# An attention and expert-layer kernel on one core: products of a cleared tile and a new order of all steps

## The chip, the cores and the metric

The kernel runs on one core of one Trainium2 chip. Five engines with queues of their own take part: TensorE (PE) multiplies matrices, VectorE (DVE), ScalarE (ACT) and GpSimd (POOL) work on tiles, and SyncE (SP) issues all loads and stores. The metric is the device time of one execution in microseconds; lower is better.

## The reference

For 4 batches of 8 heads, 768 tokens and 64 channels per head, each token attends to the keys less than 16 positions away and to 24 summaries of the whole sequence, one per block of 32 tokens (the largest key per channel, the mean of the values). The heads together are the 512 channels of a token mixer of rank 32 and a layer with 2048 hidden units.

```python
k_sum = k.reshape(B, H, nb, block, D).max(axis=3)
v_sum = v.reshape(B, H, nb, block, D).mean(axis=3)
mask_l = np.abs(pos[:, None] - pos[None, :]) < window
scores_s = scale * np.einsum('bhsd,bhnd->bhsn', q, k_sum) + np.log(block)
a = softmax([where(mask_l, scale * q @ k.T, -1e9), scores_s])
x = a @ [v, v_sum]              # (4, 768, 512) over all heads
u = x + ((x.T @ U) @ V).T       # U, V mix the tokens
out = u + np.maximum(u @ w_ch1, 0.0) @ w_ch2
```

U, V and both weight matrices arrive as 64-bit numbers, and the kernel itself turns them into 32-bit ones.

## The kernel before

The four batches follow one another. Each has an attention part and an expert layer, and the attention of batch b+1 is spread over the expert layer of batch b, so that only batch 0's attention stands alone; it is called the opening here.

**Opening.** For each of the 8 heads: load K (`.lk`) and Q (`.lq`, two transfers), take block maxima of K on VectorE (`.K`) and spread them beside the keys (`.Kd` on VectorE, `.Kp` on GpSimd), multiply Q and K by 24 small products on TensorE (`.S`, line 475), take the masked maximum on VectorE (line 500) and the exponential on ScalarE (line 510), six tiles a head (`.E`), transpose on TensorE (`.T`, line 584), copy on ScalarE (`.C`, line 590), multiply by V (`.V`, line 600) and normalise on VectorE (`.N`, lines 628 to 630). Values come in pairs of heads (`.lv`). Block means of V are products (`.M`, line 398), are taken out by ScalarE (`.Mo`) and are spread by copies on GpSimd or VectorE (`.B`, `.D` with p or d; line 438). The queries of heads 4 to 7 are loaded into the places of heads 0 to 3, so their load waits until the scores of that earlier head are done.

**Weights.** A word of 64 bits is scaled on ScalarE (`.X` for U and V, `.Z` and `c` for weights; line 243), turned in three integer steps on GpSimd or VectorE (`.Xt`, `.Y`, `t`; lines 263 to 272), and split into a high and a low part (`.Xs`, `.Xl`, `.W`, `x`; lines 287, 288). `W`, `.la`, `.lb` load a tile of weights.

**Mixer and expert layer.** U and V act through `.I`, `.J`, `.Q`; `.G` forms u for a half of the tokens and a quarter of the channels, and `.Go` takes it out, the high half on ScalarE (line 715), the low half on VectorE (line 716). The first up product (`.U0.0`, line 1018) reads all four of the first half. In batch 0, 16 weight tiles go by two halves of tokens: 12 up products (line 1018), a gate (lines 1030, 1031), and 9 down products (line 1040). The sums of weights that later batches use are formed in this time too (`w`, `d`; lines 872 to 1001) and stored. Batches 1 to 3 use fewer products by a recombination of halves (line 1290), batches 1 and 2 have plain down products (line 1386) and batch 3 a recombined second half (line 1488).

**What sets the order.** It is written out by hand in the text `PLAN`. Its words are steps; each engine's queue takes its instructions in the order of the words and waits only for the data and places that an instruction needs. A `/` ends the list of steps that stands between two groups of products of the expert layer: `body` reads one list after each group. The first list is the whole opening. TensorE's results lie in one of eight banks (`bank`).

```python
    def go():
        for word in next(plan).split():
            name = word.rstrip("0123456789.")
            words_of[name](*map(int, filter(None, word[len(name) :].split("."))))
```

Of the kernel before, what the change touches and what calls it, by code (L numbers as in the profile page):

```python
# [18 lines left out]
P = 128  # L19
# [65 lines left out]
    E1.1.0.1 a1.0.1 S1.1.1 U3 a1.0.1 c1.5 s1.0 E1.1.0.2 E1.1.1.2 t4 E1.1.1.0 t4 W1.6 W0.7
    E1.1.1.1 t4 / f1.0 a1.1.0 x1.3 / k1.3 c1.4 Ka1.2 T1.1 t5 U0 Ba1.0.1 l1.1.1 Ba1.1.1 x0.4 K1.3
    d1.0 / Ba1.0.0 S1.2.0 q1.3 / Ba1.1.0 s1.1 E1.2.0.2 D2 W0.8 W1.7 c0.7 t6 D1 E1.2.0.0 t5 U4
    S1.2.1 E1.2.0.1 q1.4 E1.2.1.1 t7 d1.1 t6 E1.2.1.2 t6 t5 E1.2.1.0 t5 Us1 f1.1 k1.4 t5 / x0.5
    w2.0 / x1.4 P1.0 N1.0 Ka1.3 / S1.3.0 / t6 t6 t6 x1.5 W0.9 a1.1.0 c1.6 c0.8 a1.1.0 t7 t7 T1.2
    Ds1 t8 E1.3.0.1 W1.8 a1.1.0 w2.1 s1.2 / E1.3.0.2 D5 c1.8 v1.3 E1.3.0.0 W1.9 / S1.3.1 q1.5  # L90
    E1.3.1.0 x0.6 k1.5 v1.2 E1.3.1.1 E1.3.1.2 U5 a1.1.0 d2.0 W0.10 t7 c1.7 c0.9 t7 P1.1 N1.1
    K1.4 / T1.3 f1.2 d2.1 a1.1.1 a1.1.0 D3 Ba1.2.1 R1.0 Ka1.4 t7 x0.7 t8 / / / Ba1.2.0 x1.6
    c0.10 c1.9 D6 S1.4.0 E1.4.0.1 U7 w3.0 E1.4.0.0 a1.1.0 t8 K1.5 / / t9 a1.1.1 E1.4.0.2 a1.1.1
    Ka1.5 a1.1.1 t8 r1.0 S1.4.1 E1.4.1.0 E1.4.1.1 P1.2 s1.3 E1.4.1.2 w3.1 Ds2 N1.2 a1.1.1 t8
    W0.11 t8 / / t10 W1.10 t9 t9 a1.1.1 S1.5.0 q1.6 d3.0 g1.0 T1.4 x1.7 x0.8 / E1.5.0.0 E1.5.0.2
    t9 d3.1 E1.5.0.1 / t9 / f1.3 a1.1.1 c0.11 S1.5.1 / Ba1.3.0 t10 Ba1.3.1 Us2 D7 E1.5.1.2
    E1.5.1.0 a1.1.1 s1.4 k1.6 U9 P1.3 E1.5.1.1 W0.12 t10 t9 W1.12 t11 x0.9 N1.3 x1.8 U8 T1.5 t10
    t10 / M1.0 / t10 K1.6 c0.12 R1.1 v1.5 x0.10 D4 w4.0 c1.10 W0.13 Mo1.0 / W1.11 t11 d4.0 J1.0
    x1.9 t12 Jo1.0 t11 c1.12 v1.4 r1.1 D8 t11 w4.1 c1.11 Ka1.6 k1.7 / / S1.6.0 t12 W0.14 t11 t12
    c0.13 E1.6.0.1 E1.6.0.2 a1.1.1 E1.6.0.0 x0.11 Us3 d4.1 t11 / / K1.7 O1.0.0 U10 Ba1.4.1 x1.10  # L100
    / S1.6.1 E1.6.1.2 t12 t13 E1.6.1.1 Ba1.5.1 t13 w5.0 t12 U6 / D10 / E1.6.1.0 t12 g1.1 w5.1
    O1.0.1 f1.4 Ba1.4.0 W1.14 s1.5 t13 O1.0.1 O1.0.1 O1.0.1 x1.11 / c0.14 U11 O1.0.2 d5.0 q1.7
    Ka1.7 t14 d5.1 T1.6 / x0.12 Ba1.5.0 O1.0.1 P1.4 N1.4 / / t13 k2.0 W1.13 c1.13 D11 O1.0.3
    O1.0.3 t13 O1.0.2 O1.0.1 D9 O1.0.2 O1.0.2 Us4 t14 Us5 O1.0.2 O1.0.2 / S1.7.0 c1.14 E1.7.0.0
    E1.7.0.1 W0.15 t13 v1.6 O1.0.2 / Ba1.6.1 s1.6 Ba1.6.0 f1.5 U13 E1.7.0.2 l2.0.0 Ds4 W1.15
    O1.0.3 t14 x1.12 O1.0.3 c0.15 K2.0 / O1.0.2 S1.7.1 O1.0.3 / E1.7.1.1 E1.7.1.0 P1.5 t15 w6.0
    x0.13 t14 E1.7.1.2 O1.0.3 f1.6 t14 T1.7 s1.7 w6.1 / / N1.5 t14 x0.14 c1.15 Kd2.0 x1.13 R1.2
    / Ds3 v1.7 P1.6 t15 k2.1 d6.0 a2.0.0 t15 N1.6 Ba1.7.1 f1.7 / t15 r1.2 t15 t16 Ba1.7.0 t15
    t16 / P1.7 / x1.14 N1.7 M1.2 F F R1.3 g1.2 w7.0 r1.3 t16 Mo1.2 d6.1 Us6 g1.3 p0 / O1.0.2
    J1.2 / p0 a2.0.0 Jo1.2 O1.1.0 p1 p1 x0.15 w7.1 x1.15 D12 p0 / F D15 O1.1.1 O1.1.1 U12 p0  # L110
    O1.1.1 / O1.1.2 p1 O1.1.2 O1.1.1 O1.1.1 l2.0.1 U15 O1.1.2 d7.0 F O1.1.2 / p0 a2.0.0 O1.1.2
    D14 O1.1.1 / O1.1.3 d7.1 O1.1.2 O1.1.3 O1.1.2 O1.1.3 / n0.1 O1.1.2 / O1.1.3 O1.1.3 p1 O1.1.2
    p0 n0.2 q2.0 n0.0 K2.1 a2.0.0 a2.0.0 n1.1 / / n1.2 U14 / a2.0.0 a2.0.1 o0.1 v2.0 D13 q2.1
    a2.0.1 a2.0.0 p1 a2.0.1 Kd2.1 o0.0 o0.2 Us7 O1.1.3 p0 S2.0 Ds5 o0.0 p1 E2.0.0.0 k2.2
# [1540 lines left out]
```

## Time and profile before

| | us |
|---|---|
| median of 3 runs | 630.4 (627.52 to 630.51) |
| the profiled execution | 628.68 |
| its span, from the first to the last instruction | 626.9 |
| busy: TensorE / VectorE / ScalarE / GpSimd | 604.8 / 448.0 / 351.5 / 338.9 |
| first scores begin | 5.62 |
| first up product begins | 50.44 |

The rows of a profile name a line of the kernel, an engine, an operation and what it writes and reads (out<-in) with sizes; `xN` is a count. In a timeline the first number is the start, the second the length of what was merged into the row, and the bracket tells how long the engine was idle before it and what ended that. "PEld" is TensorE's loading of stationary operands, "SPq" the queue of transfers. In the windows each engine has its busy time in a stretch.

### The profile page before, as it was taken

Reading aid. Unit: us, or ns where it says so; the run is one execution under the profiler, and the core shown is the slowest. Engines: PE = TensorE matmul, PEld = TensorE weight load, DVE = VectorE, ACT = ScalarE, POOL = GpSimd, SP = SyncE. Lnnn points to the kernel's source line nnn. Section 1 sums busy time; section 2 is a strip of 40 time slices with the busy share of each in tenths; the row PEclk is TensorE's granted clock in tenths of the full one; section 3 lists DMA queues with packets and bytes.
Section 4 is the critical chain, followed back from the end, with each engine's and each line's share of the span. In section 5 each row is a group of like instructions: output and inputs, shape, how many; then the busy total and the mean of one; then the engine's idle time right before and its main releaser. Section 6 shows DMA issues by size and latency. Waiting matters only on the chain.

```text
span 626.9 us, 14659 instructions
## 1 busy us (share of the span) xinstructions
PE 604.8 (96%) x5360; PEld 551.7 (88%) x5360; DVE 448.0 (71%) x1174; ACT 351.5 (56%) x796; POOL 338.9 (54%) x383
## 2 busy tenths in 40 slices
...
GB/s 231 219 348 248 319 295 290 295 251 282 309 287 242 302 260 284 252 291 250 202 278 174 163 192 235 194 270 211 306 220 263 249 188 123 136 155 264 118 179 64
DMA packets 96838, 147.89 MB, mean 236 GB/s; under 512 B 9472, under 2 KB 67200, under 8 KB 96768
## 3 DMA queue, kind: packets, MB, share of 16 engines
...
HBM read 104.46 MB, written 42.47 MB: 234 GB/s over the span
## 4 chain that ended last, share of the span: by engine, by line
PE 85%; DMA 4%; SPq 3%; DVE 3%; issue 2%; POOL 1%; ACT 1%; DVEq 0%; ACTq 0%; POOLq 0%
PE ps_h L1290 27%; PE acc L1386 19%; PE ps_h L1018 10%; PE acc L1040 9%; PE accx L1488 4%; PE accy L1488 3%; PE accz L1488 3%; PE ps_x L614 2%; PE ps_s L475 2%; DMA place<-in_q 2%; PE ps_s L452 2%; DMA there<-squares 1%; SPq L323 1%; SPq L978 1%; DMA place<-in_w 1%
## 5 line engine op out<-in xcount | busy, mean ns | idle before, releaser
L968 POOL TENSOR_TENSOR parts<-whole,parts 128x512 fp32r<-128x512 f32 (+1 forms) x128 | 158.8, 1253 | 114.4 <-ACT parts L964 98.0
L1290 PE MATMUL ps_h<-place,parts 128*128 128x384 f32 x1008 | 179.9, 336 | 1.0 <-DVE o L1063 0.8
L1290 PEld LDWEIGHTS ps_h<-place,parts 128*128 128x128 f32 x1008 | 174.4, 188 | 3.5 <-DVE o L1063 1.1
L1386 PE MATMUL acc<-gh,parts 128*128 128x256 f32 (+1 forms) x512 | 134.0, 341 | 0.0
L1386 PEld LDWEIGHTS acc<-gh,parts 128*128 128x128 f32 x512 | 88.7, 189 | 12.3 <-issue 1.2
L964 ACT CAST parts<-whole 128x512 fp32r<-128x512 f32 (+1 forms) x144 | 80.4, 581 | 18.3 <-DMA whole<-dsum 5.8
L1386 PE MATMUL acc<-gl,parts 128*128 128x512 f32 (+1 forms) x256 | 86.5, 338 | 0.0
L510 ACT ACTIVATE e<-e,neg 128x120 f32<-128x120 f32 x144 | 51.2, 389 | 42.5 <-DVE neg L500 39.3
L1018 PE MATMUL ps_h<-place 128*128 128x384 f32 x384 | 74.0, 341 | 1.1 <-DVE x L630 0.7
L1018 PEld LDWEIGHTS ps_h<-place 128*128 128x128 f32 x384 | 66.9, 188 | 3.8 <-issue 1.3
L1040 PE MATMUL acc<-place,gh 128*128 128x512 f32 x192 | 66.4, 400 | 0.0
L1359 ACT ACTIVATE gh<-place 128x768 fp32r<-128x768 f32 x32 | 27.1, 846 | 60.6 <-PE acc L1386 60.5
L263 POOL TENSOR_SCALAR val<-place 128x512 f32<-128x512 f32 (+1 forms) x30 | 47.8, 1602 | 21.9 <-ACT place L243 14.7
L288 POOL TENSOR_TENSOR place<-val,place 128x512 fp32r<-128x512 f32 x29 | 39.4, 1366 | 31.0 <-ACT place L287 28.0
L1386 PEld LDWEIGHTS acc<-gl,parts 128*128 128x128 f32 x256 | 48.5, 189 | 4.6 <-DVE gl L1364 0.4
L1364 DVE SCALAR_TENSOR_TENSOR gl<-place,gh 128x768 fp32r<-128x768 f32 x32 | 32.3, 1009 | 27.0 <-ACT gh L1359 27.0
L1040 PEld LDWEIGHTS acc<-place,gh 128*128 128x128 f32 x192 | 36.1, 188 | 7.2 <-ACT gh L1030 0.2
L500 DVE CUSTOM_DVE_ANT_0 e<-ps_s,mask_sb 128x120 f32<-128x120 f32 x144 | 35.1, 275 | 7.8 <-PE ps_s L452 4.4
L1040 PE MATMUL acc<-place,gl 128*128 128x512 f32 x96 | 37.9, 395 | 0.0
L1319 DVE TENSOR_TENSOR place<-place,ps_h 128x384 f32<-128x384 f32 x24 | 13.2, 551 | 28.2 <-PE ps_h L1290 28.1
L744 POOL TENSOR_TENSOR place<-tmp,place 128x384 fp32r<-128x384 f32 x24 | 26.8, 1126 | 11.0 <-ACT place L740 10.8
L530 DVE STREAM_TRANSPOSE squares<-e 128x768 f32<-128x768 f32 x24 | 23.3, 972 | 12.9 <-ACT e L510 8.4
...
## 6 DMA issues: line engine op xcount, KB each, us to landing
...
there<-squares SPq DMA_DIRECT2D x24, 384.0 KB, 4.7
at<-there SPq DMA_DIRECT2D x96, 96.0 KB, 3.5
whole<-up SPq DMA_DIRECT2D x24, 384.0 KB, 3.7
...
kt<-in_k SPq DMA_DIRECT2D x24, 288.0 KB, 4.1
```

Of the source, the lines that this page charges most:

```text
L263: nc.gpsimd.tensor_scalar(f32(bits), f32(hi), 0.0, None, ALU.mult)
L288: engine.tensor_tensor(lo, val, f32(hi), ALU.subtract)
L500: nc.vector.tensor_tensor_reduce(out=e[:, u, :], in0=ps[:, i * KC : (i + 1) * KC], in1=mask_sb[:, m, :], scale=-SCALE, scalar=BIG, op0=ALU ...
L510: nc.scalar.activation(e[:, u, :], e[:, u, :], AF.Exp, bias=st.neg[h][:, u : u + 1], scale=-1.0,)
L964: nc.scalar.copy(hi, whole)
L968: (nc.vector if key[0] == "second" else nc.gpsimd).tensor_tensor(lo, whole, f32(hi), ALU.subtract)
L1018: nc.tensor.matmul(ps[:, :NH], w_split[0, f][:, c % 2, part_w, c // 2], ut[c], start=(n == 0), stop=(n == 3 * NC - 1),)
L1040: nc.tensor.matmul(acc[t], gt[:, sl], w_split[1, f][:, part_w], start=(first and j == 0), stop=(last and j == 2),)
L1290: nc.tensor.matmul(ps, a[:, sa, i], b[i][:, sb], start=(first and n == 0), stop=(n == 5), skip_group_check=not first,)
L1364: nc.vector.scalar_tensor_tensor(gl, h, 0.0, f32(gh), ALU.max, ALU.subtract)
L1386: nc.tensor.matmul(place, w[:, part_w, c * P : (c + 1) * P], gt[:, q0:q1], start=(f == 0 and i == 0 and j == 0), stop=(f == NF - 1 and j = ...
L1488: nc.tensor.matmul(ps, w[j][:, sa, c * P : (c + 1) * P], gate[sb], start=fresh and q == 0 and j == 0 and k == 0, stop=q == 3 and j == 1 an ...
```

## The change

A tile of 128x128 numbers is cleared by GpSimd at the start; it takes one of the two places that batches 1 to 3 use for K (`kt`). A new step `.w` multiplies it with 120 of its own columns, n times, into a bank that nobody reads. `PLAN` has six `.w1` and three `.w4`: three single ones ahead of the first scores, two `.w4` between the third and the fourth head, the rest later in the opening, and the last `.w1` between the first groups of products of batch 0's expert layer. All other words are the same, each as often as before, in the same number of lists, in a new order throughout. The first lists and one place of batch 3 (the steps `M3.2`, `Mo3.2` and `J3.2`) are shown.

```diff
--- before
+++ after
 PLAN = """
-    .lm .lk0 .lq0 .lk3 .lu .li .lq3 .X .K0 .Kd0 .S0 .K3 .Kd3 .E1.0 .E1.1 .E1.2 .lk2 .Xt0 .lk1
-    .S3 .E0.0 .E0.1 .E0.2 .K2 .lq2 .E7.0 .E7.1 .E7.2 .Kp2 .lq1 .S2 .E6.0 .E6.1 .E6.2 .T6 .E4.0
-    .E4.1 .E4.2 .K1 .T1 .F .Xt1 .T0 .T4 .Kp1 .lv0 .lv1 .C0 .lk5 .S1 .C6 .lk6 .E5.0 .E5.1 .E5.2
-    .T5 .lq5 .E2.0 .E2.1 .E2.2 .C1 .M0 .E3.0 .E3.1 .E3.2 .T7 .K5 .Xt2 .T2 .Kp5 .Mo0 .Bp3 .T3
-    .Bd2 .Xs .lq6 .K6 .C2 .Dp0 .C4 .Dp3 .lk4 .Bp1 .Dp1 .C5 .Kd6 .S5 .C7 .V1 .lk7 .V4 .lq4 .Bp0
-    .C3 .Dp2 .E10.0 .E10.1 .E10.2 .E11.0 .E11.1 .E11.2 .S6 .V2 .Xl .K4 .E12.0 .E12.1 .E12.2 .V0
-    .lq7 .V5 .V7 .V3 .lv2 .lv3 .Kp4 .K7 .Kp7 l1.0.0 .z0 .z1 .E13.0 .E13.1 .E13.2 .S4 .N1 .E8.0
-    .E8.1 .E8.2 .T10 a1.0.0 .V6 .E9.0 .E9.1 .E9.2 .la0 a1.0.0 .S7 .T11 .N2 .E14.0 .E14.1 .E14.2
-    .T12 .la3 .T13 .Q1 .E15.0 .E15.1 .E15.2 .N0 .M1 .Mo1 .C11 .N3 .Bp5 .I0 .Bd6 .T8 .la1 .Dd5
-    .lr .Z0 .Io0 .C10 .Dp4 .T15 .lb0 .Y0.0 .T9 .Y0.1 a1.0.0 .Bp4 .Dp7 .C8 k1.0 .T14 .V10 .V11
-    .Y0.2 .C9 .Dp6 .la4 .C14 .V9 .C13 q1.0 .Bp7 .C12 a1.0.0 .N5 .V8 .V12 .C15 .N4 .V13 a1.0.0
-    .V15 c0.3 .V14 .N6 .J0 a1.0.0 .Z1 .lb1 .Q0 .N7 a1.0.0 .Jo0 .I2 .Qo0 .lb2 .Io2 .Y1.0 .G0.0
-    .Qo1 .J2 .G1.0 .Y1.1 .lb4 .G0.1 .G1.1 .Go0.0 .Jo2 .G0.2 t3 .G0.3 .W0 .Go0.1 .Go1.1 .G1.3
-    .Go0.2 .Go0.3 .Y1.2 .Go1.3 .G1.2 c0.4 c1.2 .Go1.0 .Go1.2 .W1 .lb3 .U0.0 .la2 w0.0 t3 .Z2 t2
-    K1.0 l1.0.1 / w0.1 / t2 t2 t2 k1.1 a1.0.1 t2 t2 / v1.1 W0.5 t3 Ka1.0 x1.1 t3 q1.1 x0.2
...
+    .lm .lk2 .w1 .lk1 .lk3 .lk0 .lq3 .K2 .K1 .w1 .K3 .Kd3 .w1 .lq0 .K0 .lq1 .Kp1 .lq2 .S3 .E7.2
+    .S1 .li .E6.1 .Kd0 .Kp2 .E3.0 .E6.0 .E7.0 .lv1 .S2 .w4 .lv0 .E4.0 .lk5 .E7.1 .E2.0 .E6.2
+    .lk6 .E5.2 .lk7 .E4.1 .w4 .lq5 .E3.1 .E2.2 .E3.2 .S0 .T7 .lu .E2.1 .C7 .E4.2 .F .E1.0 .lq6
+    .M0 .E1.2 .E0.0 .E5.0 .Mo0 .T3 .E1.1 .E5.1 .lk4 .lq7 .K5 .T5 .T1 .lq4 .T4 .T2 .C3 .E0.1 .Bp3
+    .E0.2 .lv2 .C5 .lv3 .C1 .T6 .K6 .la0 .Bd2 .C4 .w1 .Kd6 .Dp3 .C6 .V7 .Dp2 .C2 .K7 .X .Kp5
+    .Dp1 l1.0.0 .S5 .E10.0 .V6 .Dp0 .E11.1 .E10.2 .V4 .T0 .E10.1 .C0 .S6 .E11.0 .Kp7 .Bp1 .N3
+    .E13.0 .K4 .Bp0 .E13.2 .Xt0 .E11.2 .la1 .E12.0 .E13.1 .E12.2 .E12.1 .Kp4 .Xt1 .V0 .S7 .lb0
+    .E14.2 .V1 .V2 .S4 .E14.1 .V5 .E15.2 .lr .Xt2 .w4 .E9.1 .E9.2 .E14.0 .V3 .Xs .E9.0 .T12 .N0
+    .E15.1 .T10 .E8.2 .E8.0 .T11 .T14 .E15.0 .T9 .E8.1 .C10 .Xl .M1 .C11 .N1 .N2 .Mo1 .T13 .Dd5
+    .Bp5 .lb1 .Z0 .Dp6 .T8 .C13 .Bd6 .V11 .V10 .Dp4 .Bp4 .T15 .C12 .Y0.0 .N5 .C9 .Bp7 .Y0.1 .V13
+    .C8 .V12 .V9 .I0 .V8 .C14 .Dp7 .V14 .C15 .la3 .la2 .Io0 .V15 .N6 .N4 .N7 l1.0.1 .Z1 .J0 .Q0
+    .Y1.0 .I2 .Q1 .Jo0 .Io2 .Qo0 .J2 .G0.1 .Qo1 k1.0 .Y0.2 a1.0.0 a1.0.0 a1.0.1 .Y1.1 .Jo2 .z0
+    .G0.0 .G1.0 .lb3 .Go0.1 .G0.2 .Z2 .G0.3 .Y1.2 .G1.2 .Go0.0 .G1.3 c0.3 .Go0.2 .lb2 .W0 .Go0.3
+    .w1 .G1.1 .Go1.2 .la4 a1.0.0 .Go1.0 .Go1.1 .Go1.3 t2 .U0.0 .W1 t2 / a1.0.1 / K1.0 t2 v1.1
+    w0.0 w0.1 c1.2 / .lb4 t2 c0.4 v1.0 t2 t3 a1.0.0 t2 D0 t3 d0.0 a1.0.0 W0.5 a1.0.0 Ka1.0 q1.0
+    .w1 / c1.4 a1.0.1 a1.0.0 k1.1 q1.1 K1.1 Us0 U2 t3 t3 x1.1 / / x0.2 c1.3 Ka1.1 S1.0.1
+    E1.0.1.2 D1 E1.0.1.0 W0.6 t4 l1.1.0 E1.0.1.1 .z1 t3 t3 a1.0.1 / d0.1 t4 / c0.6 S1.0.0 / t4
...
@@ batch 3, around its mixing product
-    N3.7 O3.0.1 p1 G11 G12 p0 / p0 / M3.2 / Mo3.2 p1 h2.13 G6 / J3.2 R3.3 y2.12 G9 r3.3 Jo3.2
...
+    O3.0.3 / / g3.2 / O3.0.2 N3.7 G11 / / O3.0.2 / / M3.2 O3.0.1 y2.11 O3.0.1 / F O3.0.2 Mo3.2
+    y2.12 p1 / R3.3 / J3.2 / p1 p0 G7 r3.3 / / p1 Jo3.2 O3.0.1 O3.0.2 / O3.0.2 h2.13 p0 G9 h2.14
...
@@ set-up of batch 0
     raw_uv = weight_place(0, 2, I32)[:, : 4 * NU * R]
 
+    spin = kv.tile([P, KTW], F32, name="kt")[:, :P]
+    nc.gpsimd.memset(spin, 0.0)
     nc.gpsimd.memset(means_w, 0.0)
...
+    def keep_busy(n):
+
+        ps = bank("ps_w")
+        for _ in range(n):
+            nc.tensor.matmul(ps[:, :KC], spin, spin[:, :KC], start=True, stop=True)
...
         "N": lambda h: normalise(st, h),
+        "w": keep_busy,
         "F": mean_weights,
```

In the new order K of four heads is loaded ahead of the first queries, the heads go 3, 1, 2, 0 instead of 0, 3, 2, 1, the loads of U and V and their scaling stand later, and the split of the up weights of tile 2 (`x0.2`) stands in the seventh list instead of the fourth.

More of the change, by code (lines that the diff above doesn't have):

```diff
@@ L85 @@
[L85 to L114, printed above, removed]
@@ new lines @@
+    x1.2 E1.0.0.2 a1.0.1 E1.0.0.1 E1.0.0.0 t4 U0 x0.3 T1.0 Ds0 / k1.2 a1.0.1 K1.2 W1.5 S1.1.0
+    W1.6 Ka1.2 E1.1.0.0 q1.2 / D2 E1.1.0.1 c0.5 S1.1.1 E1.1.0.2 t6 t4 E1.1.1.1 a1.0.1 E1.1.1.0
+    t4 s1.0 k1.3 x1.3 q1.3 E1.1.1.2 W0.7 w1.0 a1.1.0 f1.0 / a1.0.1 / T1.1 w1.1 d1.0 W0.8 t5 x0.4
+    a1.0.1 W1.7 / S1.2.0 c0.7 E1.2.0.2 E1.2.0.1 t5 U3 D3 K1.3 U1 Ba1.0.0 Ka1.3 E1.2.0.0 t5 /
+    S1.2.1 E1.2.1.2 c1.5 t5 t5 E1.2.1.1 / / k1.5 t6 q1.4 Ba1.0.1 c1.6 E1.2.1.0 P1.0 a1.1.0 t5
+    Ba1.1.1 t6 N1.0 s1.1 x1.4 x0.5 T1.2 Ba1.1.0 W1.8 U5 t7 c0.8 / S1.3.0 E1.3.0.2 w2.0 l1.1.1
@@ new lines @@
+    W0.11 x0.9 T1.4 a1.1.1 / N1.2 / a1.1.1 U9 S1.5.0 E1.5.0.0 r1.0 S1.5.1 D8 E1.5.0.1 x1.8
+    E1.5.0.2 a1.1.1 E1.5.1.1 E1.5.1.2 c0.11 E1.5.1.0 P1.3 c0.12 K1.6 t10 q1.6 N1.3 R1.1 k1.7
+    d3.0 t10 / t10 d3.1 t10 r1.1 M1.0 W0.13 t10 s1.4 Mo1.0 U8 Ka1.6 t10 / / J1.0 d4.0 Jo1.0
+    c1.11 t11 t11 / D7 x1.9 x0.10 K1.7 g1.0 t11 T1.5 t12 S1.6.0 W1.13 t12 c0.13 t11 / c1.13
+    E1.6.0.2 E1.6.0.0 a1.1.1 E1.6.0.1 / d4.1 v1.5 t12 O1.0.0 a1.1.1 W1.12 t11 t11 w4.0 / x0.11
+    Us3 a1.1.1 x1.10 S1.6.1 E1.6.1.0 E1.6.1.2 E1.6.1.1 v1.4 / s1.5 g1.1 w5.0 t12 w4.1 / Ba1.4.1
```

153 lines of the change are left out of this document (84 added, 69 removed).

## The prediction

> **What bounds the kernel now.** I read the page's head first, then the busy time by stage, then TensorE's waits, then the timelines of the opening.
>
> ```profile
> span 626.9 us, 14659 instructions
> ...
> PE 604.8 (96%) x5360; PEld 551.7 (88%) x5360; DVE 448.0 (71%) x1174; ACT 351.5 (56%) x796; POOL 338.9 (54%) x383
> ```
>
> TensorE is busy for 604.8 of 626.9 us, so a new order of the same work can give back at most some 22.1 us. Where they lie is shown by the busy time of each engine in six stretches: the opening (attention of batch 0), the rest of batch 0 with batch 1's attention, batch 1, batch 2, and batch 3 in two parts.
>
> ```profile
> core 0: us, PE busy (x) PEld busy (x) DVE busy (x) ACT busy (x) POOL busy (x), PEclk, DMA share, GB/s
> 0.00:50.44 50.44, 36.72 (x740) 30.03 (x741) 35.35 (x173) 31.30 (x87) 23.78 (x56) 1.00 0.93 275
> 50.44:209.35 158.91, 156.45 (x1205) 138.91 (x1205) 141.94 (x335) 89.66 (x210) 111.41 (x104) 1.00 0.91 281
> 209.35:361.06 151.71, 150.81 (x1415) 135.93 (x1414) 106.53 (x278) 85.49 (x185) 91.04 (x110) 1.00 0.78 243
> 361.06:506.50 145.44, 144.04 (x1334) 130.40 (x1333) 84.12 (x240) 81.09 (x176) 76.94 (x85) 1.00 0.76 234
> 506.50:562.70 56.20, 56.20 (x326) 56.20 (x325) 28.84 (x48) 37.85 (x84) 35.76 (x31) 1.00 0.47 144
> 562.70:626.90 64.20, 60.57 (x349) 60.24 (x347) 51.17 (x104) 26.16 (x55) 0.00 (x0) 1.00 0.49 161
> ```
>
> TensorE is idle for 13.7 us in the opening, then for 2.5, 0.9, 1.4 and 0.0 us, and for 3.6 us at the end, where the last output leaves. Only the opening has much to give. No engine is full in it; the transfers are, at 0.93 of their time. After 50.44 us VectorE comes second, at 141.94 of 158.91 us (89%). TensorE's largest named waits, and those of the later stretches:
>
> ```profile
> PE ps_s L475 <- DMA place<-in_q: 9.3, 6, 5.6
> PE ps_s L452 <- ACT gh L1030: 1.4, 1, 1.4
> PE ps_r L661 <- ACT t L656: 1.2, 1, 1.2
> PE ps_h L1290 <- DVE o L1063: 0.8, 1, 0.8
> PE ps_h L1018 <- DVE x L630: 0.7, 1, 0.7
> ```
>
> The first is batch 0's scores waiting for their queries. L452 and L1018 belong to the second stretch, L1290 and L661 to later batches.
>
> **The cleared tile's products.** Six steps of one and three of four add 18 products of a 128x128 with a 128x120 tile; 17 stand in the opening, one in batch 0's expert layer. The scores of batch 1 have the same sizes:
>
> ```profile
> L452 PE MATMUL ps_s<-kt,qz 128*128 128x120 f32 x96 | 13.3, 274 | 1.4 <-ACT gh L1030 1.4
> ```
>
> 13.3 us / 96 is 0.14 us each at the fast clock, 0.28 us at half of it: 2.4 us for the 17 in one case, 4.8 us in the other. That time is covered by TensorE's 13.7 idle us of the opening; if the cover were gone, it would cost itself. The one at the expert layer costs 0.14 us on the path. The tile also holds one of the two K places of batch 1 until that last product; the load of its second K (`k1.1`) waits for it on the queue, but stands right behind it and is needed three step pairs later.
>
> Does it change the clock? TensorE's score rows of the opening, and the first up product:
>
> ```profile
> 5.62 0.63 PE L475 MATMUL ps_s<-place 64*64 64x120 f32 x2 [5.62 <-DMA place<-in_q]
> 6.41 1.47 PE L475 MATMUL ps_s<-place 64*64 64x120 f32 x22 [0.17 <-DMA place<-in_q]
> 9.39 1.78 PE L475 MATMUL ps_s<-place 64*64 64x120 f32 x24 [1.51 <-DMA place<-in_q]
> 12.61 1.80 PE L475 MATMUL ps_s<-place 64*64 64x120 f32 x24 [1.44 <-DMA place<-in_q]
> 17.19 0.84 PE L475 MATMUL ps_s<-place 64*64 64x120 f32 x22 [0.33 <-POOL place L434]
> 29.38 0.87 PE L475 MATMUL ps_s<-place 64*64 64x120 f32 x24
> 50.44 4.38 PE L1018 MATMUL ps_h<-place 128*128 128x384 f32 x24
> ```
>
> A head's scores take 1.8 us until 14.4 us and half of that from 17.2 us on, though the column of the granted clock reads 1.00 throughout. [...] In the new order three single products come ahead of the first scores. They wait for nothing but the clearing of their tile, so TensorE does them back to back in the first 3 us, 3 x 0.28 = 0.8 us of work, and is then idle until the first head's loads land. I take no gain from them. [...]
>
> [...]
>
> **The opening.** Loads are issued from one queue in the order of the steps, so what has landed is told by the kilobytes ahead.
>
> ```profile
> place<-in_k SPq DMA_DIRECT2D x8, 288.0 KB, 5.0
> place<-in_q SPq DMA_DIRECT2D x16, 96.0 KB, 4.4
> place<-in_uv SPq DMA_DIRECT2D x1, 384.0 KB, 5.0
> mask_sb<-in_mask SPq DMA_DIRECT2D x1, 240.0 KB, 2.8
> ident_sb<-in_ident SPq DMA_DIRECT2D x1, 64.0 KB, 4.7
> ```
>
> Before: the first head needs mask, K and both halves of Q, 240 + 288 + 192 = 720 KB, and starts at 5.62 us; the third (`.S2`) starts at 12.61 us with 2416 KB asked for up to its queries. That is 1696 KB in 6.99 us, 243 KB/us. After: K of four heads goes ahead of the first queries, so `.S3` needs 240 + 4 x 288 + 192 = 1584 KB and starts at 5.62 + 864/243 = 9.2 us, 3.6 us later than any score now. `.S1` and `.S2` need 1968 and 2160 KB (10.8 and 11.6 us) and follow without a pause, each 1.8 us or less: `.S2` ends by 14.6 us. With 8 filling products (1.1 to 2.2 us) and `.S0` at 0.9 us, four heads are done at about 17 us, where `.S1`, now the fourth, ends at 18.0. So the late start is made good, and 1 us more. The queue of loads also loses a stall:
>
> ```profile
> SPq L323 <- PE ps_s L475: 4.6, 1, 4.6
> ```
>
> Head 5's queries reuse head 1's place and wait today for `.S1`, ordered fourth; in the new order `.S1` is second.
>
> What comes next, though, is ScalarE and VectorE. In the stretch of the softmaxes, and in the one behind it up to the first up product:
>
> ```profile
> 8.95:33.31 24.36, 20.80 (x432) 16.67 (x432) 18.87 (x128) 18.44 (x60) 11.94 (x32) 1.00 0.91 234
> 32.39:50.70 18.31, 14.90 (x318) 12.81 (x311) 14.48 (x38) 12.30 (x31) 8.72 (x15) 1.00 1.03 364
> ```
>
> ScalarE works 18.44 us from the first exponential to the last. In the new order the scaling of U and V (0.55 us, now before it) joins in: 19.0 us. The first exponential cannot come before 9.2 + 1.8 = 11.0 us, nor the last end before 30.0 us; with today's 5.9 us of waits it would end at 35.9. GpSimd decides between them, since the spreading of the last head's maxima (`.Kp4`) now stands behind seven copies of value means, two other spreads and `.Xt0`:
>
> ```profile
> 9.13 1.20 POOL L263 TENSOR_SCALAR val<-place 128x384 f32<-128x384 f32 x1 [5.48 <-ACT place L243]
> 19.96 1.46 POOL L434 COPY place<-km 64x48 f32<-64x48 f32 x4 [2.83 <-DVE km L417]
> 20.50 0.19 ACT L410 COPY vsum<-ps_n 128x65 f32<-128x65 f32 x1
> 21.48 3.99 POOL L438 COPY place<-vsum 24x390 f32<-24x390 f32 x7
> ```
>
> 4.0 + 3 spreads of 1.0 to 1.5 + 1.2 is 8.2 to 9.7 us behind the block means, which are taken out at 20.5 us today and hardly earlier in the new order, since the exponentials ahead of them start later: the last scores start at about 29 us, 0.4 us before today's (29.38), and the last exponential ends near 33 us instead of 33.3. The clearing of the new tile is one more memset on GpSimd, covered by the 5.48 us that it waits ahead of 9.13 us.
>
> VectorE then has today 14.48 busy us, to the end of the fourth low half that the first up product reads. New on it: the low half of V and one conversion step, gone one low half:
>
> ```profile
> 24.10 0.45 DVE L1110 TENSOR_TENSOR place<-val,place 128x192 fp32r<-128x192 f32 x1
> 50.62 1.28 DVE L272 SCALAR_TENSOR_TENSOR val<-place,val 128x512 int32<-128x512 int32 x2
> L716 DVE TENSOR_TENSOR place<-ps_u,place 128x384 fp32r<-128x384 f32 x5 | 2.6, 555 | 0.4 <-ACT place L715 0.4
> ```
>
> 14.48 + 0.45 + 1.28 - 0.56 = 15.65 us. Its last softmax work ends 0.9 us ahead of the last exponential today. From 30.0 - 0.9 us without any wait the 15.65 us end at 44.8; from 35.9 with today's 3.8 us of waits at 55.4; from 32.5 with half the waits, midway between the ends, at 50.0. Today they end at 50.7. The opening gives **-0.7 us**, bounds -5.9 and +4.7.
>
> **After the opening.** One up and one down product take
>
> ```profile
> 66.86 2.11 PE ps_h L1018 x12
> 68.96 2.09 PE acc L1040 x9
> ```
>
> so a step pair is 4.2 us. TensorE has 2.5 idle us there, all on VectorE's and ScalarE's conversions and softmaxes. The new order has the weights of tile 2 split one step ahead of their product instead of four, those of tile 9 four instead of two; slack is taken from the start and given to the middle, where the 1.4 and 0.7 us of waits lie. I take -0.5, between -2.5 (all waits go) and +5.0 (the lost lead of three steps, 6.3 us, less the 1.3 us of conversion that now precede the layer). For L661, batch 3's mixing product stands one step further behind the copy it waits for: -0.5 of 1.2. For the other later waits 0, between -0.8 and +2. In the last two stretches TensorE never pauses and the end is one output's way out: 0.
>
> Sum: 628.68 (the profiled execution: span 626.9, 1.8 around it) - 0.7 + 0.1 - 0.5 - 0.5 = 627.1 us. The median of the runs shown, 630.4, lies 1.7 above that execution, which would make it 628.8. I say **628 us**.
>
> **Rivals.** (1) *The stall of the load queue was the real limit.* For: 4.6 us, and transfers at 0.91 of their time in the softmax stretch. Then VectorE starts at 30.5, half a microsecond above its bound, ends at 30.5 + 15.65 + 1.9 = 48.0 (-2.7), and the conversions arrive ahead of need (-2.5): 628.7 - 2.7 - 2.5 - 1.2 = 622.3. Against: ScalarE's 19.0 us start 2.4 us later than now. (2) *VectorE falls behind in batch 0's expert layer.* It has 17 us free in 158.9. If its steps run a step pair (4.2 us) late when tile 2 is due, its split stands too near to its product to hide that, and what TensorE loses there isn't regained, as TensorE has no spare time later. The price is the whole lost lead: 628.7 + 5.0 = 633.7. For: 89% busy, and a lead of one step. Against: one conversion step more is done before. (3) *The clock was on the path.* If the cleared products do hold the fast clock, the three slow heads lose 0.9 us each: 628.7 - 2.8 = 625.9. Against: loads set their starts, and the idle time before the first.
>
> **Chances.** A comparison of this kernel tells no less than 0.5% from no change: below 627.2 is faster, above 633.6 slower. My forecast gets 0.50 (0.10 of it faster, 0.38 same, 0.02 slower), with a range of its own of 625.5 to 631.5; rival 1 0.18 (faster); rival 2 0.24 (0.17 slower, 0.07 same); rival 3 0.08 (0.07 faster, 0.01 same). Sum: faster 0.35, same 0.46, slower 0.19. The range that leaves out 2 in 10 runs from 621.5, past rival 1, to 635.5, past rival 2.
>
> **What would show it.** In the profile after: 18 new products, the first three before 3 us; the first score group at 9.2 us and at 1.8 us for 24; four heads done near 17 us; no wait of 4.6 us at L323; the last exponential at 33 us; the first up product at 50 us, 48 to 52. Idle TensorE of 1 to 3 us between there and the end of batch 0. The forecast is wrong if the first up product moves by over 2 us, or if a wait on VectorE's conversions (L269 to L272, L997 to L1001) passes 4 us.

## The result, and the profile after

The changed kernel is slower: 636.9 us at the median of 20 runs (631.48 to 639.84) against 630.33 us, a ratio of 1.0087 with a 95% interval of 1.0062 to 1.0113. The prediction was 628.0 us; the time lies above the range, which ended at 635.5. The kernel before also ran 128 times beside the experiments; three of these runs, over 1.5% above its fastest, are left out of every comparison below. The profiled execution took 635.08 us, 633.0 of them span; before it was 628.68 with a span of 626.9, so 6.1 us are to be found in the trace. Both are quick executions, 1.7 and 1.8 us under their medians.

The busy time by the same six stretches as before, each ending at the same product (columns: stretch, length, busy us of each engine with its instructions, granted clock, share of the transfers):

```profile
core 0: us, PE busy (x) PEld busy (x) DVE busy (x) ACT busy (x) POOL busy (x), PEclk, DMA share, GB/s
0.00:51.73 51.73, 39.74 (x774) 33.84 (x775) 34.97 (x172) 30.82 (x87) 21.95 (x53) 1.00 0.90 279
51.73:211.85 160.12, 156.90 (x1207) 139.44 (x1207) 138.95 (x337) 89.81 (x211) 110.58 (x106) 1.00 0.90 278
211.85:365.20 153.35, 152.11 (x1416) 135.58 (x1415) 107.97 (x280) 85.45 (x186) 92.23 (x113) 1.00 0.76 231
365.20:512.90 147.70, 145.52 (x1333) 131.51 (x1332) 83.41 (x238) 82.02 (x177) 75.72 (x85) 0.99 0.77 237
512.90:569.10 56.20, 56.20 (x326) 56.20 (x325) 31.11 (x48) 36.13 (x80) 37.46 (x31) 1.00 0.47 146
569.10:633.00 63.90, 60.54 (x348) 60.22 (x347) 50.78 (x102) 27.02 (x57) 0.00 (x0) 0.99 0.50 162
```

Against before the lengths differ by +1.29, +1.21, +1.64, +2.26, 0.00 and -0.30 us. No single stretch has the loss. In the first, TensorE is 3.0 us longer busy (39.74 against 36.72) and its idle time falls by only 1.7 us. TensorE's waits (line, released by, total us, times, longest):

```profile
PE ps_s L475 <- DMA place<-in_q: 6.6, 1, 6.6
PE ps_x L614 <- DMA at<-there: 2.6, 3, 1.9
PE ps_x L600 <- issue: 2.1, 1, 2.1
PE ps_s L475 <- DMA qz<-in_q: 1.8, 1, 1.8
PE ps_m L643 <- issue: 1.6, 1, 1.6
PE ps_w L1139 <- POOL kt L1088: 1.0, 1, 1.0
...
PE ps_r L661 <- ACT t L656: 0.4, 1, 0.4
```

The waits on VectorE and ScalarE that the prediction spoke of are gone or smaller; in their place stand two loads (`at<-there`, `qz<-in_q`) and two pauses marked "issue" (2.1 and 1.6 us, 1.6 and 1.0 before), in which TensorE waited for nothing that the profile shows. TensorE in the opening, with the cleared products at L1139:

```profile
0.99 1.64 PE L1139 MATMUL ps_w<-kt 128*128 128x120 f32 x6 [0.99 <-POOL kt L1088]
9.19 4.18 PE L475 MATMUL ps_s<-place 64*64 64x120 f32 x72 [6.56 <-DMA place<-in_q]
13.30 2.51 PE L1139 MATMUL ps_w<-kt 128*128 128x120 f32 x16
15.74 0.84 PE L475 MATMUL ps_s<-place 64*64 64x120 f32 x24
...
29.26 1.15 PE L1139 MATMUL ps_w<-kt 128*128 128x120 f32 x8
```

The first scores start at 9.19 us and the fourth head is done at 16.6. A cleared product has two records: six for the three first ones, sixteen for the eight behind the third head. The four at 29.26 us, all at full clock, take 0.29 us each; of the eight, the first two still run at half of it (their records start 0.21 us apart, the later ones 0.11). In the groups of the first 33.4 us (busy us, mean ns of a record):

```profile
L1139 PE MATMUL ps_w<-kt 128*128 128x120 f32 x32 | 5.7, 331 | 1.0 <-POOL kt L1088 1.0
```

5.7 - 1.64 = 4.1 us for the 13 that run there after the first scores, 0.31 us each on the mean. With them the stretch in which they stand is full:

```profile
11.00:33.40 22.40, 21.72 (x457) 18.45 (x453) 19.25 (x132) 19.55 (x62) 7.75 (x20) 1.00 0.98 290
```

Without them it isn't: the first row is the kernel before, the second e1 below, the new order without the products. TensorE has 3.1 and 3.4 us left there (2.4 to 3.8 in the four kernels without products), less than the 4.1 us that they take.

```profile
11.00:33.30 22.30, 19.18 (x411) 15.26 (x408) 17.61 (x117) 16.63 (x53) 10.74 (x31) 1.00 0.89 228
11.00:33.40 22.40, 19.00 (x397) 15.94 (x389) 17.30 (x120) 17.80 (x56) 7.58 (x20) 0.85 0.97 272
```

### The profile page after: what moved, and what is told of

Its sections match the earlier page's. It is cut to its first block, busy times and chain, and to the rows that moved or that the text cites. A ratio compares the mean times of both kernels' runs of the same rounds, so it can differ in the third digit from the quotient of the medians.

```text
span 633.0 us, 14754 instructions
## 1 busy us (share of the span) xinstructions
PE 611.0 (97%) x5396; PEld 556.8 (88%) x5396; DVE 447.2 (71%) x1174; ACT 351.2 (55%) x796; POOL 337.9 (53%) x384
## 4 chain that ended last, share of the span: by engine, by line
PE 73%; DMA 12%; DVE 5%; SPq 4%; issue 3%; POOL 3%; ACT 1%; POOLq 0%; DVEq 0%; ACTq 0%
PE acc L1395 19%; PE ps_h L1299 19%; PE ps_h L1018 8%; PE acc L1040 7%; PE accx L1497 4%; PE accy L1497 3%; PE accz L1497 3%; PE ps_x L614 3%; DMA at<-there 3%; DMA place<-in_k 2%; DMA whole<-up 2%; DMA there<-squares 2%; PE ps_s L475 2%; DMA whole<-down 1%; POOL parts L968 1%
## 5 line engine op out<-in xcount | busy, mean ns | idle before, releaser
L1299 PE MATMUL ps_h<-place,parts 128*128 128x384 f32 x1008 | 181.9, 337 | 1.0 <-POOL parts L968 0.5
L288 POOL TENSOR_TENSOR place<-val,place 128x512 fp32r<-128x512 f32 x29 | 39.7, 1372 | 28.6 <-ACT place L287 25.3
L744 POOL TENSOR_TENSOR place<-tmp,place 128x384 fp32r<-128x384 f32 x24 | 28.4, 1188 | 14.5 <-ACT place L740 14.4
L1030 ACT ACTIVATE gh<-ps_h 128x384 fp32r<-128x384 f32 x32 | 15.7, 491 | 36.5 <-PE ps_h L1018 36.3
L1360 DVE TENSOR_TENSOR place<-place,ps_h 128x384 f32<-128x384 f32 x24 | 13.3, 552 | 31.9 <-ACT place L1359 31.9
```

What stands on the lines that cost most here:

```text
L288: engine.tensor_tensor(lo, val, f32(hi), ALU.subtract)
L1299: nc.tensor.matmul(ps, a[:, sa, i], b[i][:, sb], start=(first and n == 0), stop=(n == 5), skip_group_check=not first,)
```

## The experiments

The theory was at first that three things add up: the products' time on a full TensorE, the new waits for loads, and a fall of the clock behind each pause. Each kernel ran beside the kernel before on one chip; the sixteen were spread over three chips. The table puts the results in one place; the texts follow. "Clock" is the mean granted clock over the runs. The last column is the mean time against before's with both brought to one clock: within each kernel, over 325 runs, the time rises by 0.49 us for each 0.001 of clock (standard error 0.04), and that part is taken off; ± is the standard error of the difference.

| kernel | products | ratio to before, 95% interval | clock | at one clock, us |
|---|---|---|---|---|
| before | 0 | 1 | 0.998 | 0 |
| e1, new order alone | 0 | 1.0013 [0.999, 1.0036] | 0.9967 | +0.5 ± 0.6 |
| f1, with the tile | 0 | 0.9999 [0.9977, 1.0021] | 0.9970 | 0.0 ± 0.5 |
| f3, with tile and banks | 0 | 1.0006 [0.9976, 1.0036] | 0.9963 | +0.4 ± 0.6 |
| e5, e1 with waits moved | 0 | 1.0014 [0.9994, 1.0034] | 0.9970 | -0.1 ± 0.6 |
| e7, first three | 3 | 1.0059 [1.0035, 1.0083] | 0.9969 | +2.6 ± 0.4 |
| g3, the three later | 3 | 1.0043 [1.001, 1.0075] | 0.9947 | +1.0 ± 0.6 |
| g4, the three doubled | 6 | 1.0039 [1.001, 1.0068] | 0.9957 | +1.0 ± 0.5 |
| e6, without the eight | 10 | 1.0070 [1.0043, 1.0097] | 0.9942 | +2.3 ± 0.5 |
| g2, without the first three | 15 | 1.0048 [1.0023, 1.0073] | 0.9963 | +2.3 ± 0.6 |
| f2, no banks for them | 18 | 1.0048 [1.0021, 1.0076] | 0.9960 | +2.2 ± 0.5 |
| a2, the change again | 18 | 1.0092 [1.0068, 1.0117] | 0.9943 | +3.4 ± 0.5 |
| e3, change with `q3.4` ahead | 18 | 1.0034 [1.0011, 1.0058] | 0.9962 | +1.5 ± 0.6 |
| e4, change with its wait filled | 18 + 6 | 1.0060 [1.0038, 1.0082] | 0.9947 | +2.0 ± 0.4 |
| e2, order of before | 18 | 1.0048 [1.0028, 1.0068] | 0.9978 | +3.1 ± 0.5 |
| f4, order of before, no banks | 18 | 1.0055 [1.0028, 1.0083] | 0.9962 | +3.1 ± 0.5 |
| g1, order of before, first three | 3 | 1.0037 [1.001, 1.0064] | 0.9976 | +2.1 ± 0.5 |

**The two halves of the change.** e1 takes the tile, its clearing and all `.w` steps out of the changed kernel; e2 puts them into the order of before.

```
e1:  - spin = kv.tile([P, KTW], F32, name="kt")[:, :P]
     - nc.gpsimd.memset(spin, 0.0)
     - every .w1 and .w4
e2:  + the tile and keep_busy;  .lk0 .w1 .w1 .w1   .S2 .w4 .w4   .w1 .S5   .S7 .w4   .w1 .G1.2   and .w1 ahead of k1.1
```

> The new order without the cleared tile and its 18 products. Theory A (the order costs the time: transfers that land late in the middle of the kernel): hardly better than the changed kernel, ratio to before 1.006 to 1.009; the wait of about 1.8 us for queries near 417 us stays. Theory B (the cleared products cost it: two records each, some 5 us of TensorE time, and they shift everything behind them): ratio 1.000 to 1.002. In the opening the clock would reach full speed 1 to 2 us later than with the products.

> The order of before with the cleared tile and its 18 products, put where they stand in the new order: three ahead of the first scores, eight behind the third head, five later in the opening, one ahead of the last mixing product and one in batch 0's expert layer (the last two are not covered by idle time: 0.3 us each). Theory A: ratio 0.999 to 1.002, first up product within 1 us of 50.4 us. Theory B: ratio 1.005 or more, with the first up product 3 us later or waits behind it that before has not.

The order alone is worth nothing either way (1.0013); the products with their tile cost 0.5% in the order of before. So it is the part that was costed at nothing that costs. At one clock the halves add up, 0.5 and 3.1 us against the 3.4 us of a2; the rest of the changed kernel's loss is clock (0.9943 in a2, 0.9967 and 0.9978 in the halves). Two expectations missed. In e1 the clock rose no later than with the products: records shorten from 0.40 to 0.26 us at 13.2 us, in the changed kernel from 0.42 to 0.27 us at 14.3 us. And in e2 the first up product comes 1.1 us later, not 3:

```profile
14.29 3.50 PE L1137 MATMUL ps_w<-kt 128*128 128x120 f32 x16
...
51.51 1.74 PE L1016 MATMUL ps_h<-place 128*128 128x384 f32 x9
```

So in the order of before the opening takes in most of the products' time, and still the kernel loses; where is taken up below.

**The wait at 415 us.** In the changed list the queries of head 4 of batch 3 (`q3.4`) stand behind a gather (`f3.1`), a load of V and one of K; the chain of waits of the changed kernel shows the queue and then TensorE (columns: start, us, what):

```profile
409.57 0.04 issue
409.62 0.43 SPq L337
...
411.06 0.48 SPq L930
411.54 0.04 issue
411.59 5.22 DMA qz<-in_q
416.81 0.14 issue
416.94 1.90 PE ps_s L475 x24
```

The clock beside it, in stretches of 2 us:

```profile
414.00:416.00 2.00, 1.13 (x50) 0.73 (x48) 0.00 (x0) 0.00 (x0) 0.15 (x1) 1.00 1.07 287
416.00:418.00 2.00, 1.06 (x15) 0.85 (x19) 0.00 (x0) 1.29 (x3) 0.59 (x1) 0.77 0.91 355
418.00:420.00 2.00, 2.00 (x21) 1.70 (x15) 0.53 (x1) 1.38 (x5) 1.91 (x2) 0.50 0.68 270
420.00:422.00 2.00, 2.00 (x12) 2.00 (x11) 1.52 (x4) 1.04 (x3) 0.37 (x1) 0.88 0.76 189
```

The slice that lies whole in the fall reads 0.50, so 0.77, 0.50 and 0.88 are 0.92 + 2.00 + 0.48 = 3.4 us at half clock. e3 moves `q3.4` ahead of `f3.1`; e4 leaves the wait and fills it with six products of the identity that nobody reads.

```
e3:  - ... f3.1 / y2.1 v3.3 k3.5 ... F ... q3.4      + ... q3.4 f3.1 / y2.1 v3.3 k3.5 ... F ...
e4:  + .k6 ahead of S3.4:  nc.tensor.matmul(ps[:, :KC], ident_sb, ident_sb[:, :KC], ...)  six times
```

> The changed kernel with one step moved: the queries of head 4 of batch 3 are asked for ahead of the fetch of head 1's turned exponentials instead of behind it, two loads and two more transfers. Theory A with the clock (the wait of 1.8 us and the half clock for 3.4 us that follows cost 3.5 us together): no wait at these scores, no fall of the clock near 417 us, ratio to before 1.002 to 1.005. Rival (the transfers are the limit there, and the wait passes to the next transfer, the fetch that now stands behind): a wait of 1 us or more at the values of head 1, ratio 1.007 to 1.009.

> The changed kernel with six products of the identity put between the values of head 1 and the scores of head 4 of batch 3, into the 1.8 us in which TensorE waits for queries; nobody reads them. The wait itself stays. Theory of the clock (a window with too little TensorE work halves the clock for 3.4 us, 1.7 us of work lost): the clock doesn't fall near 417 us, 1.5 to 2 us less than the changed kernel, ratio 1.005 to 1.007. Rival (idle time is all that counts, the half clock is covered or comes anyway): ratio 1.008 to 1.010.

Both times came out as expected, in e4's profile the clock stays at 1.00 from 410 to 424 us, and the same stretch of e3 has neither the wait nor the fall:

```profile
416.00:418.00 2.00, 2.00 (x75) 1.57 (x74) 0.00 (x0) 0.00 (x0) 0.10 (x1) 1.00 0.75 220
418.00:420.00 2.00, 2.00 (x12) 1.81 (x11) 0.00 (x0) 1.32 (x3) 0.62 (x1) 1.00 1.03 415
```

One profile of each can't show more than that the fall is possible, nor that too little work is what brings it. Eleven kernels of the new order keep the wait (1.4 to 2.6 us in their profiles); the clock falls behind it in seven of them, and not in a2, which is the changed kernel itself and waits 1.73 us.

**Do the parts add up?** a2 is the changed kernel once more, for comparison; e5 takes the products away, moves `q3.4` ahead and moves a mean (`F`) and a load (`l2.0.0`) behind the gather `f1.7`, for which TensorE waits in the changed kernel:

```profile
193.37 0.89 PE L614 MATMUL ps_x<-vt,at 120*32 120x65 f32 x48 [1.87 <-DMA at<-there]
```

```
e5:  - spin = kv.tile(...), its memset, every .w step
     - ... f3.1 / y2.1 v3.3 ... F ... q3.4          + ... q3.4 f3.1 / y2.1 v3.3 ... F ...
     - l2.0.0 ... F in the list ahead of f1.7        + f1.7 F l2.0.0
```

> The changed kernel as it is, beside the three others on one chip. If comparisons across chips hold, the ratio to before is 1.006 to 1.011; if what the first runs without the cleared products showed was the chip, it is 1.000 to 1.004.

> The new order without the cleared tile, and with two waits taken away: the queries of head 4 of batch 3 are asked for ahead of the fetch of head 1's turned exponentials, and a load of weight sums and one of values of batch 2 stand behind the last fetch of batch 1 instead of ahead of it. If the two causes add up (cleared products some 4.7 us, the wait for queries with the clock's fall 3.4 us), the ratio to before is 0.994 to 0.998; if the wait only looked like a cost beside the products, it is 1.000 to 1.003.

They don't add up to the 0.994 to 0.998 of the first theory. With the products, `q3.4` ahead seems to save 0.5% (1.0034 against 1.0087); without them both moves together show no gain (1.0014 against e1's 1.0013), though the second had nothing to save there: TensorE waits for no gather in that place in e1, f1 and f3. Each of these differences is known to some 0.3%, so that the saving differs with the order is likely, not shown.

**Which products?** e6 and e7 leave parts of them out.

```
e6:  - .w4 behind .S2, - .w4 behind .E4.1
e7:  - all .w steps but the three .w1 ahead of .S3
```

> The changed kernel without the eight cleared products between the third and the fourth head; the ten others stay. If products cost their time where TensorE is full (from 9 to 33 us it is busy for 97% of the time), 2.5 us go: ratio 1.003 to 1.006. If the tile's place in the ring of K tiles, its bank or the shift of the program behind it is what costs, nothing changes: 1.007 to 1.010.

> The changed kernel with only the three cleared products ahead of the first scores; tile, clearing and bank stay. If products cost their time where TensorE is full, these three are free, as TensorE waits for loads until 9 us: ratio 0.999 to 1.003, as without any. If the tile or the bank costs: 1.005 or more.

e7 went against the theory of time on a full TensorE: three products that run at 1 to 2.6 us, when TensorE has nothing to do, cost as much as half of the change. e6, at 1.0070, lies between its two theories, and its interval reaches into both. That left the tile (it takes a K place of batch 1), its clearing, and the nine banks of PSUM that the calls take, by which the turn of the eight banks shifts for all that follows. f1 has the tile without products, f3 also takes the banks, f2 and f4 let the products write into the bank that the next step takes anyway:

```
f1:  the tile and its memset kept, every .w step out
f3:  def keep_busy(n):  bank("ps_w")                    (no product)
f2:  def bank(name):  return lent.pop() if lent else psum.tile(...)    and in keep_busy:  lent.append(ps)
f4:  f2's edit on e2
```

> The changed kernel with the cleared tile (its place in the K ring, so that K of batch 1 takes the places the other way round, and its clearing on GpSimd) but without any of the 18 cleared products; no step of the reference is left out. Theory P (the products cost, by their time on TensorE and by the pauses they make of what comes after): as the new order without tile and products, 1.0013, so 1.000 to 1.003 of the kernel before. Theory B (each call of the products takes a bank of PSUM and so turns the order of the eight banks for all that follows): no bank is taken here, so 1.000 to 1.003 too. Theory K (the place in the K ring or the clearing costs): 1.004 to 1.008, the share that the three first products with the tile showed over the new order alone.

> The changed kernel with its 18 cleared products, but they write into the bank that the next step takes anyway (whose first product starts that bank anew), so that no bank is taken for them and the order of the banks is that of the kernel before. Theory P (time of the products): as the changed kernel, 1.007 to 1.011. Theory B (turn of the banks): 1.001 to 1.004. Theory K (place in the K ring): as the changed kernel, 1.007 to 1.011.

> The changed kernel with the tile and with the nine banks taken where the products took them, but without the products; no step of the reference is left out. Theory P: 1.000 to 1.003. Theory B: 1.004 to 1.009, since the turn of the banks is that of the changed kernel. Theory K: 1.004 to 1.008, and then the kernel with the tile alone shows it too.

> The order of before with the 18 cleared products (1.0048 in the run that took banks for them), now written into the bank that the next step takes anyway. Theory P: 1.003 to 1.007. Theory B: 1.000 to 1.002. Theory K: 1.003 to 1.007. The products leave out nothing of the reference, and nobody reads them.

In the new order neither place nor clearing nor banks cost (0.9999, 1.0006), and in the order of before the banks don't (1.0055 without against 1.0048 with them); the tile without products was not run in that order. f2, at 1.0048, came out below what each theory that clears the banks expected; its interval reaches to 1.0076. So in the new order the products themselves cost. The last four runs asked again for the three first:

```
g1:  order of before, .w1 .w1 .w1 behind .lk0, no other
g2:  the changed list without its three first .w1
g3:  only three .w1, behind .K2, the tile cleared by VectorE there
g4:  the three first as .w2, no other
```

> The order of before, with only the three first cleared products (with the tile and its clearing); nothing of the reference is left out. Theory A (the three first products cost by themselves, as the 1.0059 of the changed order with them alone against some 1.0006 of it without any says): 1.003 to 1.006. Theory B (a product costs only where TensorE is full; the three first run in its first 3 us, when it has nothing else, and the 1.0059 was the spread of eight runs): 0.999 to 1.002.

> The changed kernel without the three first cleared products, with the 15 later ones; nothing of the reference is left out. Theory A: the changed kernel's 1.009 less the 0.004 to 0.005 of the three, 1.003 to 1.006. Theory B: as the changed kernel, 1.006 to 1.011, since the 15 at 0.29 us are 4.3 us on a TensorE that is busy 97% of the time from 11 to 33 us.

> The changed order with three first products alone, but their tile is cleared by VectorE behind the first maxima of K, so that they run at some 5 to 7 us in place of 1 to 2.5 us, still ahead of the first scores; nothing of the reference is left out. Theory A, if the early start of TensorE is what costs: 0.999 to 1.002; if it is the products as such: 1.004 to 1.007. Theory B: 0.999 to 1.003.

> The changed order with the three first calls alone, each of two products in place of one (six in all, from 1 to some 4 us, ahead of the first scores); nothing of the reference is left out. Theory A, if the cost goes by the number of products: 1.009 to 1.012; if by their being there at all: 1.004 to 1.007. Theory B: 0.999 to 1.003.

The three do cost something (1.0037 to 1.0059 in four kernels and both orders; without products the new order lies at 0.9999 to 1.0014), and not by their number: six stand at 1.0039, where 1.009 or more was expected if the number counts. Whether their early start matters is open. The later three (g3) stand at 1.0043, but at one clock they and the six cost 1.0 us, within two errors of the -0.1 to 0.5 us without any. The 15 others cost 0.4 to 0.5% alone, and 0.9% stands with all.

**Where it goes, as far as the traces show.** All kernels of the new order have the same products but for the cleared ones, so the time from the first score to the 720th other record, a little ahead of the first up product, can be compared directly, one profiled execution of each. The changed kernel's fall behind its wait for `q3.4` is one piece of 3.41 us, from 417.07 to 420.48 us (0.50 there, 1.00 on both sides). 3.41 us at half clock are 0.0027 of the mean clock of a run, so 0.49 us per 0.001 makes them 1.33 us, an estimate; that is taken off for each such piece in the stretch.

| kernels | from first score to record 720, at one clock | pause near record 590 |
|---|---|---|
| no products: f1, e1, f3, e5 | 36.8, 36.6, 36.4, 37.1 us | 1.54, 1.54, 1.81, 1.31 us |
| three or six, all first: e7, g3, g4 | 37.1, 36.7, 37.2 us | 1.79, 1.36, 1.37 us |
| e6, ten (seven after the first scores) | 37.5 us | 1.97 us |
| with the eight: g2, after, a2, f2, e3, e4 | 39.4, 39.8, 38.9, 40.2, 39.7, 39.7 us | 2.11, 2.12, 2.39, 2.38, 2.10, 2.11 us |

With the later products the opening is 2.9 us longer (39.6 against 36.7), out of the 4.1 us that they take there. From record 720 to the end the same kernels differ by no more than their spread.

The delay doesn't stand where the products do. At one clock the six kernels with the eight lie 2.6 us behind the four without any where the eight have just run (record 72), and only 0.1 ± 0.2 us behind at record 130: pauses that the four have there take the eight in. By record 230 they are 1.8 us behind, and still are at record 550 (1.8 ± 0.2). The pause near record 590, longer in them, makes it 2.5, and 2.9 stand at record 720.

In the order of before the same count gives 42.3 us, 43.2 and 43.1 us with the 18 products (e2, f4) and 42.4 us with three (g1): at most 1.0 us in the opening, for 2.1 to 3.1 us in the time. Their profiles are longer behind it. Batch 1 takes 154.9, 154.2 and 158.7 us against 151.7 in the kernel before, with TensorE idle for 3.5, 2.8 and 5.9 us against 0.9. Why products of the opening, or the tile that comes with them, should cost there isn't known.

The pauses with no releaser, in the changed kernel's timeline:

```profile
36.62 0.45 PE L600 MATMUL ps_x<-place 120*64 120x65 f32 x7
39.19 1.05 PE L600 MATMUL ps_x<-place 120*64 120x65 f32 x29 [2.12 <-issue]
...
43.46 0.82 PE L643 MATMUL ps_m<-x,u_sb 128*32 128x128 f32 x18
45.91 0.31 PE L643 MATMUL ps_m<-x,u_sb 128*32 128x128 f32 x3 [1.64 <-issue]
```

Where the eight products stand the clock stays up, at 1.00 from 16 to 24 us in the changed kernel. In e1, without any, four heads' scores end at 14.0 us, two pauses follow, and the clock falls:

```profile
9.27 4.73 PE L473 MATMUL ps_s<-place 64*64 64x120 f32 x96 [9.27 <-DMA place<-in_q]
14.17 0.74 PE L582 MATMUL ps_t<-ident_sb,gl 128*120 128x128 f32 x3 [0.17 <-ACT gh L508]
16.13 0.44 PE L396 MATMUL ps_n<-place,means_w 96*32 96x65 f32 x16 [1.22 <-DVE means_w L387]
18.22 2.40 PE L396 MATMUL ps_n<-place,means_w 120*32 120x65 f32 x80 [1.66 <-DMA place<-in_v]
```

The clock of e1 in that place:

```profile
16.00:18.00 2.00, 0.44 (x16) 0.27 (x16) 1.57 (x15) 2.00 (x8) 0.00 (x0) 0.66 1.07 331
18.00:20.00 2.00, 1.78 (x68) 1.81 (x72) 1.01 (x6) 0.51 (x2) 0.00 (x0) 0.50 1.09 304
20.00:22.00 2.00, 2.00 (x31) 1.56 (x23) 1.54 (x5) 1.31 (x5) 0.92 (x2) 0.50 1.07 314
22.00:24.00 2.00, 2.00 (x13) 1.95 (x11) 1.19 (x4) 1.83 (x5) 1.71 (x6) 0.63 0.63 173
```

0.68 x 2 + 2 + 2 + 0.74 x 2 = 6.8 us at half clock. In the profiles of the new order the clock falls between 16 and 19 us in six of the eight kernels without the eight products, and in none of the six with them, though in two of these it falls 4 to 6 us later. But over the whole opening falls are as many with the eight as without: seven pieces of 3.4 us in six profiles against nine in eight, since the clock falls later, from 38 to 46 us, in four of the six. And they take 2.5 us to save an estimated 1.3 us for each piece. The three first leave no such mark; in g2, without them, three heads' scores run as in the changed kernel:

```profile
9.15 4.12 PE L473 MATMUL ps_s<-place 64*64 64x120 f32 x72 [9.15 <-DMA place<-in_q]
```

**What stays open.** In the timed runs the three first products cost 1.0 to 2.6 us at one clock, more than the 0.3 us that the traces show from the first score to record 720. No stretch behind it has the rest in all of e7, g3 and g4; ahead of it their first scores begin at 10.05, 8.30 and 9.83 us, where the four without products have 8.2 to 9.3, which one profile of each can't settle. What the products cost in the order of before isn't placed either. Nor is it known why `q3.4` ahead seems to save more than its wait with the products and nothing without them.

## Why the prediction was wrong, point by point

- **The step that failed is the cover of the cleared products**: "That time is covered by TensorE's 13.7 idle us of the opening". The new order without them takes as long as before (0.9999 to 1.0014); with them it loses, 2.2 to 3.4 us at one clock with 15 or 18 of them (g2, f2, a2), and 2.9 us stand at the end of the opening. The 13.7 us were the idle time of the whole opening. 5.6 of them lay ahead of the first score, and where the 13 products behind it stand, from 11 to 33.3 us, 3.1 (3.4 in e1), for products of 4.1 us. Nor does a gap that takes a product in settle its price: the eight are made good by record 130, and the opening ends 2.9 us later all the same. In the order of before it takes in all but 1.0 us, and the time still rises by 3.1 us.
- **The price of a product was halved.** "13.3 us / 96 is 0.14 us each": the 96 are records, two per product. The 13 products take 4.1 us, not the 1.8 us of 13 x 0.14. Of "if the cover were gone, it would cost itself", 2.9 of these 4.1 us came true in the opening.
- **The clock was taken as settled.** "I take no gain from them" holds for the three first: three heads' scores take 4.18 us with them and 4.12 us in g2, which has only the later ones (row above). The eight were given none either; with them the clock does stay up from 16 to 19 us (no fall in six profiles, against falls in six of eight without), though the opening as a whole has no fewer falls with them. No run shows how much work the full clock takes: the records shorten from 0.42 to 0.27 us at 15.7 us in the kernel before, 3.1 us behind the end of TensorE's last pause, and at 14.3 us in the changed kernel, 5.1 us behind it; in e1 from 0.40 to 0.26 us at 13.2 us, 3.9 us behind it. Rival 3 had a held clock, but not the products' price. What no step had is a fall of the clock later in the kernel, as behind the wait for `q3.4` in seven of eleven profiles: the mean clock falls from 0.998 to 0.994, 0.49 us x 3.7, or 1.8 us of the mean loss of 5.2 us in the second run of the change. Without the products the new order lies at 0.9967, so part of the falls belongs to the order, part to the products.
- **The order of loads and the end of the softmaxes were right**: 9.2 us for the first score (9.19), about 17 for four heads (16.6), 33 for the last exponential (32.07 + 0.38 = 32.45, row below), no wait of 4.6 us at L323 (the longest there is 1.0). But the first up product comes at 51.73, not 50.0: TensorE, not VectorE (34.97 busy us, 0.4 less than before), ends the opening, with the products and two "issue" pauses of 3.8 us together (2.6 before). The bound of +4.7 held it, but a slip stands in that sum: "from 35.9" leaves out the 0.9 us that the lower end takes off, so the terms give 54.5, a bound of +3.8, and 49.6 for the middle. The 51.73 us lie inside either.

```profile
32.07 0.38 ACT L510 ACTIVATE gh<-gh,neg 128x120 f32<-128x120 f32 x1
```

- **After the opening** -0.5 for batch 0's layer was +1.21, inside its bounds of -2.5 and +5.0 and by another cause: L452's 1.4 us went, and in this profile the gather `f1.7` came late by 1.87 us. A wait for such a gather, of 0.7 to 2.2 us, stands late in that stretch in all seven profiles of the new order with ten products or more and in none of the seven with fewer, but the stretch, between the same two products, takes 158.9 to 161.3 us in the fourteen profiles of the new order and 159.4 to 161.0 in the four without products (158.75 before). So the new order makes it longer without that wait and without the products. L661 went from 1.2 to 0.4 us, 0.8 gained where 0.5 was said. "For the other later waits 0, between -0.8 and +2" was too narrow: batches 1 and 2 grew by 1.64 and 2.26 us, the second with the wait for `q3.4` (1.81 us) and an estimated 1.3 us of clock behind it. That queue move was to be read in the list, which shows `q3.4` behind `f3.1`. All in all the order was to gain 1.7 us (0.7, 0.5 and 0.5) and gains nothing: in one profile each of the four kernels without products the opening ends at 48.1 to 51.1 us (50.4 before), but batch 0's layer, batch 1 and batch 2 take 457.6 to 462.2 us together (455.9 before).
- **The rivals.** Rival 2's 633.7 us came nearest, for another reason: VectorE is busy for 138.95 of 160.12 us in that stretch (87%) and no wait of TensorE on a conversion passes 0.2 us there. Rival 1 is refuted by e1: with the stall gone and no products, the time stays.
